# One core of attention plus a spectral mixer: placing the other work, the VectorE exponentials and the clock filler by a table of when engines and tiles come free

## The chip, the cores and the metric

The kernel runs on one core of a Trainium2 chip. The metric is the device time of one execution in microseconds. Engines are named as in the profile: PE (TensorE matmul), PEld (its weight load), DVE (VectorE), ACT (ScalarE), POOL (GpSimd), SP (SyncE, which issues most DMAs).

## What is computed

```
x: 2048 x 448;  16 heads of 28
qkv = x @ wqkv;  p = softmax(q k^T * 28**-0.5);  a = (p v) @ wo          # attention
X = rfft2(x);  X = X * (w_r + 1j*w_i);  b = irfft2(X)                    # spectral mixer
g = sigmoid(sum(x * gate_w));  out = g * a + (1 - g) * b
```

The attention has 16 heads x 2048 x 2048 exponentials. The two Fourier transforms are written as matmuls with constant matrices, 16 tiles per stage.

## The kernel before

The head loads x and the weights, transposes x, and makes the keys, the first queries and the first values. Then `attention` runs the main loop. The heads are taken four at a time (T = 0..3) and the queries 512 at a time (q = 0..3), so there are 16 chunks (T, q), and each chunk has 16 key blocks x 4 heads = 64 score tiles of 128 keys x 512 queries: 1,024 in all.

A step m of the loop handles three score tiles. `scores(m)` makes three matmuls into one PSUM tile `psS` (three banks, two such tiles in turn). `exps(m)` is one ACT instruction over the whole tile, which writes `Pt`. `values` multiplies finished `Pt` tiles by the values, eight at a time, into `psPV`. In some steps one of the three tiles is not given to ACT: `away` makes its exponential on DVE and POOL, as a chain: `bits` (DVE, reads psS), `frac` and a second `bits` (DVE), two `horner` operations on POOL, two `horner` on DVE, and `px` (DVE), which `values` then uses. The list `AWAY` gives 44 such tiles, at fixed places in each chunk, and the steps of a chain are emitted 0, 3, 4 and 5 steps after the tile.

Everything else is "other work", a list of units with due steps: the projections of the next keys and queries (`pkb`, `pn`, `pq`, `pq2`), the values (`pvp`), the Fourier stages (`psx1`, `psA`, `psT`, `psB`, `psZ`, `psY`) and the output tiles (`pf`). Each unit is a few matmuls into the one PSUM bank `bg` (`ps_bg`, one buffer), and a DVE operation that empties it. So a unit's first matmul waits until DVE has emptied the unit before.

All engines run strictly in the order of emission (`InOrder` keeps the program order). PE therefore meets, in each step: filler, scores of the next step, values, other work. The planner `other_work(m, room)` counts matmul columns: a step has `ROOM` = 1.22 us of PE time, filler, values and scores are taken off, and units are emitted while their columns fit in the rest. It knows nothing of when the bank, DVE or POOL come free. `filler` adds matmuls on a zero tile `warm`, with results that nobody reads, into the psS tile ahead of the scores; it wants 3 x `BUSY` = 4,950 columns over three steps. `need(key)` emits units without a limit when the next scores depend on them. The operations put in `later` for a step (chain steps, `normalise`) are emitted at the end of that step.

The functions that the change touches, and what calls them:

## Time and profile before

| | |
|---|---|
| runs, us | 490.14, 494.55, 493.25; median 493.25 |
| profiled execution: own time / span / granted clock | 490.54 us / 488.0 us / 0.986 |
| busy in the span | ACT 457.2 us (94%), PE 399.3 (82%), DVE 343.8 (70%), POOL 187.6 (38%) |
| start to first exponential | 18.48 us |
| first exponential to end of the last | 461.3 us (18.48 to 479.82) |
| from there to the end of the span | 8.2 us |
| exponentials on ACT | 297 of 128x1536, 44 of 128x1024, 1 of 128x512 |
| exponentials on DVE and POOL | 44 of 128x512 |
| filler matmuls in psS | 162 |

The span is what the profiler saw of one execution; that execution's own time is 2.5 us longer. Shares are averages over stages with different limits. In the lists, one row is a group of instructions: engine, operation, output <- input, shape, count, busy time, mean of one, and the idle time of the engine just before them with the instruction that ended it. Nearly every row has the line L128, a helper through which all operations are recorded, so rows are told apart by their tiles. Durations of neighbouring ACT instructions overlap a little: a 128x1536 exponential lasts about 1.45 us, but the next one starts 1.33 us after it.

### The profile page before, as it was taken

The page shows a single profiled execution, that of the slowest core. Times are in us where ns is not written, and L with a number is a line of the kernel's source. Part 1 is how long each engine was busy: PE and PEld are TensorE (multiplying, and loading weights), DVE is VectorE, ACT ScalarE, POOL GpSimd, SP SyncE. Part 2 cuts the span into 40 slices and gives each one's busy share as a digit, 9 for nine tenths or more (in the row PEclk, how much of TensorE's full clock was granted, in tenths as well). Part 3 has the DMA queues.
Part 4 walks back from the last instruction along what each step waited for, and adds up shares of the span by engine and source line. Part 5 has one row for each costly group of instructions (what it writes and reads, how often), then busy time and mean ns, then how long its engine had stood idle before and what let it go on. Part 6 is the DMA issues. An engine that isn't in the chain of part 4 may idle for free.

```text
span 488.0 us, 8101 instructions
## 1 busy us (share of the span) xinstructions
PE 399.3 (82%) x3162; PEld 148.2 (30%) x3164; DVE 343.8 (70%) x602; ACT 457.2 (94%) x364; POOL 187.6 (38%) x213
## 2 busy tenths in 40 slices
PE   8878878878898878787777778878878888888795
PEld 4422222222322233332333223333333233332221
DVE  4584766767585677877797677677867657686773
ACT  4899999999999999998999969999999899999993
POOL 3261625464222533435576652343224223222410
PEclk9999999999999999998999979999999899999999
DMA  8800000000000000001222100000000000100001
GB/s 251 198 2 1 1 1 0 1 1 1 2 1 1 1 0 1 0 10 46 51 56 51 54 2 0 3 1 11 23 22 11 23 1 31 49 13 21 20 28 48
DMA packets 15518, 12.69 MB, mean 26 GB/s; under 512 B 6984, under 2 KB 14600, under 8 KB 15480
## 3 DMA queue, kind: packets, MB, share of 16 engines
q1 hardware_dynamic: 14728, 11.91, 9.0%
q8 instruction: 24, 0.39, 0.3%
q10 hardware_dynamic: 752, 0.28, 0.2%
q14 instruction: 14, 0.11, 0.1%
HBM read 10.35 MB, written 1.84 MB: 25 GB/s over the span
## 4 chain that ended last, share of the span: by engine, by line
ACT 37%; PE 27%; DVE 20%; issue 14%; DMA 1%; POOL 0%; SPq 0%; DVEq 0%; ACTq 0%
ACT Pt L128 37%; PE psS L128 7%; PE psPV L128 6%; DVE bits L128 3%; PE psA L128 2%; DVE horner L128 2%; PE pkb L128 2%; DVE frac L128 2%; PE pf L128 2%; PE pq L128 2%; DVE U L128 2%; PE pvp L128 1%; DVE V L128 1%; DVE px L128 1%; DMA xtok<-in_A_x_dram 1%
## 5 line engine op out<-in xcount | busy, mean ns | idle before, releaser
L128 ACT ACTIVATE Pt<-psS 128x1536 bf16<-128x1536 f32 (+1 forms) x342 | 445.8, 1435 | 16.6 <-PE psS L128 15.1
L128 PE MATMUL psS<-qT,kT 32*128 32x512 bf16 x1024 | 135.9, 387 | 25.2 <-ACT Pt L128 22.7
L128 POOL TENSOR_SCALAR horner<-frac 128x512 f32<-128x512 f32 x44 | 37.3, 848 | 200.8 <-DVE frac L128 200.8
L128 PE MATMUL psPV<-Pt,vsb 128*32 128x512 bf16 x980 | 87.1, 390 | 0.1
L128 PEld LDWEIGHTS <-kT 32*128 32x128 bf16 x1024 | 38.3, 91 | 136.9 <-issue 125.7
L128 DVE SCALAR_TENSOR_TENSOR horner<-horner,frac 128x512 f32<-128x512 f32 x88 | 63.3, 719 | 2.6 <-POOL horner L128 1.8
L128 PE MATMUL psS<-warm 128*128 128x512 bf16 (+18 forms) x162 | 44.0, 325 | 17.6 <-ACT Pt L128 14.5
L128 POOL TENSOR_TENSOR horner<-horner,frac 128x512 f32<-128x512 f32 x44 | 55.7, 1266 | 3.7
L128 DVE TENSOR_SCALAR bits<-psS 128x512 int32<-128x512 f32 x44 | 30.2, 687 | 22.7 <-PE psS L128 22.5
L128 POOL TENSOR_TENSOR sq<-qr 128x512 bf16<-128x512 bf16 x16 | 19.6, 1227 | 41.7 <-DVE qr L128 41.7
L128 DVE SCALAR_TENSOR_TENSOR px<-horner,bits 128x512 bf16<-128x512 f32 x44 | 31.0, 705 | 0.6
L128 PEld LDWEIGHTS <-vsb 128*32 128x32 bf16 x1024 | 19.6, 94 | 35.3 <-issue 30.6
L128 PEld LDWEIGHTS <-warm 128*128 128x128 bf16 x188 | 17.8, 99 | 40.7 <-issue 26.5
L128 POOL TENSOR_TENSOR cm_t<-Xri,Wg 128x225 bf16<-128x225 bf16 x32 | 20.1, 648 | 15.7 <-DVE Xri L128 15.5
L128 DVE TENSOR_SCALAR frac<-bits 128x512 int32<-128x512 int32 x44 | 24.4, 554 | 0.1
L128 POOL TENSOR_TENSOR sq<-kT 128x512 bf16<-128x512 bf16 x12 | 15.7, 1304 | 20.4 <-DVE kT L128 20.3
L128 PEld LDWEIGHTS <-xT 112*128 112x128 bf16 x192 | 13.5, 97 | 24.1 <-issue 19.5
L128 DVE CAST ZT<-psZ 113x512 bf16<-113x512 f32 x16 | 11.0, 690 | 12.8 <-PE psZ L128 12.7
L128 DVE TENSOR_SCALAR bits<-bits 128x512 int32<-128x512 int32 x44 | 18.8, 427 | 1.5
L128 PE MATMUL pq<-xT,WqP 112*128 112x512 bf16 x64 | 17.9, 381 | 2.4 <-DVE V L128 0.9
L128 PE MATMUL pf<-WoP,qT 128*128 128x448 bf16 x60 | 15.1, 354 | 4.4 <-DVE part L128 1.6
L128 PE MATMUL psY<-Binv,ZT 113*128 113x448 bf16 x64 | 16.4, 367 | 2.6 <-DVE ZT L128 1.5
(90 smaller groups left out, 448.0 us busy)
## 6 DMA issues: line engine op xcount, KB each, us to landing
RBg<-cRB SPq DMA_DIRECT2D x16, 128.0 KB, 2.1
xtok<-in_A_x_dram SPq DMA_DIRECT2D x4, 448.0 KB, 4.6
out_dram<-fin SPq DMA_DIRECT2D x15, 112.0 KB, 1.7
CSg<-cCS SPq DMA_DIRECT2D x16, 96.0 KB, 1.9
Wg<-in_B_w_r_dram SPq DMA_DIRECT2D x16, 56.2 KB, 1.8
Wg<-in_B_w_i_dram SPq DMA_DIRECT2D x16, 56.2 KB, 2.0
Wqk<-in_A_wqkv_dram SPq DMA_DIRECT2D x1, 784.0 KB, 11.2
Binv<-cBinv SPq DMA_DIRECT2D x1, 448.0 KB, 13.4
```

Of the source, the lines that this page charges most:

```text
L128: return lambda *a, **k: self._tc.keep_in_program_order(f(*a, **k))
```

## The change

The planner's column count is replaced by a table, `Estimate`. At every emitted operation, `note` adds a cost (from shape and engine, by fixed formulas) to that engine's time, and records when the output is done, when inputs have been read, and so when a buffer comes free. The rest of the planner asks it:

- `other_work(m, limit)` emits a unit's next matmul only if the estimated start (PE free and the bg bank free) plus its cost is no later than `limit`, which is the estimated end of exponential m+1 less `GUARD` = 0.77 us. Several units may go into one step.
- The chain steps of `away` go into a queue. `steps_away`, called at the end of each step and after each finished unit, emits at most one, and holds it back if its input is not ready or if it would delay the emptying of the bg bank by the running unit (for at most `HOLD` steps).
- Tiles for DVE are chosen as the loop goes (`choose`): at least `GAP` = 4.2 us apart by the table, DVE free, no more than two chain steps waiting, none among the last 30 tiles of a chunk. `px` has five buffers where it had three. 39 tiles are chosen where the list had 44.
- `values` takes a `px` tile when the table says that it is ready, not a fixed eight steps later.
- `filler` wants 3,300 columns in the last 3.0 us by the table, where score matmuls count a third and value matmuls a quarter.

The core of the diff (pool wrappers that tell the table of new tiles, and renamed helpers, are left out):

```diff
-ROOM = 1.22
-ALLOW = 0.25
-SWITCH = 0.11
-BUSY = 1650
-UNIT = 1000
+BUSY = 3300
+UNIT = 400
+WINDOW = 3.0
+GUARD = 0.77
-AWAY = {c: [0, 5, 11] if c not in (7, 8) else [0] for c in range(16)}
-LAG = 8
+REST = 30
+GAP = 4.2
+HOLD = 4
+PXB = 5
...
+class Estimate:
+    def start(self, eng, names, out):
+        t = max(self.now[eng], self.free.get(out, 0.0))
+        return max([t] + [self.done[n] for n in names if n in self.done])
+    def columns(self, since):
+        return sum(c for t, c in self.moved if t > since)
+    def note(self, eng, op, args):
...
+        t = self.start(eng, ins, out)
+        late = 0.05
+        if eng == "PE":
+            kind = "u"
+            cols = P if op == "transpose" else n if len(aps) < 3 else int(np.prod(aps[2].shape[1:]))
+            cost = cols * MM
+            if aps[0].tensor.name.startswith("psS") and aps[1].shape[0] == 32:
+                kind, cost, cols = "s", 0.107, cols / 3.0
+            elif aps[0].shape[0] == 32:
+                kind, cost, cols = "v", 0.068, cols / 4.0
+            if kind == "u" and self.kind != "u":
+                cost += 0.09
+            self.kind, late = kind, 0.2
...
+        elif eng == "ACT":
+            cost, late = 0.06 + n * 0.833e-3, 0.13
+        elif eng == "DVE":
+            fast = op == "tensor_scalar" and len(aps) == 2 and aps[1].space != aps[0].space
+            fast = op == "tensor_scalar" and str(aps[1].space) == str(aps[0].space) and not fast
+            cost = 0.11 + n / (1920.0 if fast else 960.0)
+        else:
+            cost = 0.2 + n * 2.0e-3 if len(aps) > 2 else 0.13 + n * 1.3e-3
+        self.now[eng] = t + cost
...
-    def filler(self, m, room, base, ps):
-        want = 3 * BUSY - sum(self.activity[-2:]) - base - self.ahead(m, room)
-        fill = int(min(want, 900))
+    def filler(self, ps, ends):
+        t = self.est.start("PE", (), ps[:].tensor.name)
+        want = BUSY - self.est.columns(t - WINDOW)
+        fill = int(min(want, 900, (ends - t - 0.6) / MM))
...
+    def other_work(self, m, limit):
+        while True:
...
             key, g, cost = self.current
-            if cost > room:
-                break
+            if self.est.start("PE", (), self.bank) + cost > limit:
+                return
...
+    def steps_away(self, m, force=False):
+        est = self.est
+        while self.chain:
+            since, engine, ins, f = self.chain[0]
+            hold = m - since
+            t = est.start("DVE", ins, None)
+            if not force and hold < 2 * HOLD:
+                if t > est.now["DVE"] + 0.25 and t > est.now["PE"]:
+                    return
+                if self.current is not None and hold < HOLD:
+                    begun = est.start("PE", (), self.bank)
+                    if t + 0.6 > begun + self.left + 0.3:
+                        return
+            self.chain.pop(0)
+            f()
+            if not force:
+                return
...
+        def choose(m, t):
+            ci = acts[0][0]
+            if (len(self.chain) > 2 or t < self.last_away + GAP or len(out) >= PXB - 1
+                    or est.now["DVE"] > t + 0.3):
+                return None
...
+            if m + 1 in psS:
+                begin = max(est.now["ACT"], est.done[psS[m + 1][:].tensor.name])
+                limit = begin + 0.06 + len(tiles[m + 1]) * QW * 0.833e-3 - GUARD
+            else:
+                limit = est.now["ACT"]
+            self.other_work(m, limit)
+            self.steps_away(m)
```

## The prediction

> **What bounds the kernel now.** I read the page's busy table and its slices first, then the exponentials on ACT in order of time, then PE and DVE at the places where ACT had waited, then the granted clock there.

> ```profile
> PE 399.3 (82%) x3162; PEld 148.2 (30%) x3164; DVE 343.8 (70%) x602; ACT 457.2 (94%) x364; POOL 187.6 (38%) x213
> ACT  4899999999999999998999969999999899999993
> L128 ACT ACTIVATE Pt<-psS 128x1536 bf16<-128x1536 f32 (+1 forms) x342 | 445.8, 1435 | 16.6 <-PE psS L128 15.1
> ```

> ACT is the bound. It is full in nearly every slice, and where it waits, it waits for scores from PE. The span is 18.5 us of head, 461.3 us from the first exponential to the end of the last, and 8.2 us of tail. What would the middle be with no wait? In the trace the starts of undisturbed neighbours are 1.331 us apart after a 128x1536 and 0.904 after a 128x1024 (the longer "mean" is the duration, which overlaps the next). 297 x 1.331 + 44 x 0.904 + 0.5 = 435.6 us. So 25.7 us of the 461.3 are excess, and only this can be won. The page's 16.6 us of idle are less, since an idle gap counts only from the end of the duration, some 0.13 us later, and delays under 0.13 don't show.

> Where the excess lies (ACT in order of time, last bracket the idle time):

> ```profile
> 227.76 1.45 ACT L128 ACTIVATE Pt<-psS 128x1536 bf16<-128x1536 f32 x1 [1.46 <-PE psS L128]
> ...
> 280.92 2.37 ACT L128 ACTIVATE Pt<-psS 128x1024 bf16<-128x1024 f32 x2 [0.81 <-PE psS L128]
> 285.82 4.54 ACT L128 ACTIVATE Pt<-psS 128x1536 bf16<-128x1536 f32 x3 [2.54 <-PE psS L128]
> 291.30 1.45 ACT L128 ACTIVATE Pt<-psS 128x1536 bf16<-128x1536 f32 x1 [0.94 <-PE psS L128]
> ...
> 384.93 1.45 ACT L128 ACTIVATE Pt<-psS 128x1536 bf16<-128x1536 f32 x1 [1.27 <-PE psS L128]
> 387.01 1.45 ACT L128 ACTIVATE Pt<-psS 128x1536 bf16<-128x1536 f32 x1 [0.63 <-PE psS L128]
> ```

> Three bursts (with two more rows of 0.20 and 0.57 at 292.95 and 294.55) make 8.4 us of idle in 8 waits, with 0.13 each 9.5 us of excess. The other 16.2 us are some 60 delays of 0.1 to 0.6 us all over the loop. Now PE and DVE at the first two bursts:

> ```profile
> 225.79 0.57 PE L128 MATMUL pn<-sq,IS 128*128 128x512 bf16 x1 [1.71 <-DVE Xri L128]
> 284.26 0.91 PE L128 MATMUL psS<-warm 128*128 128x512 bf16 x2 [2.22 <-DVE bits L128]
> ```
> ```profile
> 223.51 1.69 DVE L128 SCALAR_TENSOR_TENSOR horner<-horner,frac 128x512 f32<-128x512 f32 x2
> 225.13 0.61 DVE L128 CAST Xri<-psB 128x450 bf16<-128x450 f32 x1
> ```

> PE isn't short of time, it stands in line: the emptying of the bg bank (Xri) queued on DVE behind two chain steps, a bg matmul on PE queued behind that, and the scores behind the matmul. The second burst is the same with `bits`, which holds the psS tile; the third is a ZT behind px, frac and bits. By the built order a step's PE work without filler is 0.84 us on average (a score matmul at 0.107, a value at 0.068, other columns at 2,400 per us), against 1.33 us of exponential, and only 8 of 341 steps hold more than 1.33.

> Then the clock around the bursts (PE busy, PEld, DVE, ACT, POOL, granted clock):

> ```profile
> 222.40:225.80 3.40, 1.69 (x19) 0.65 (x19) 3.30 (x7) 3.40 (x3) 2.18 (x3) 1.00 0.35 83
> 225.80:229.20 3.40, 3.40 (x20) 0.73 (x20) 3.33 (x7) 1.94 (x3) 2.39 (x3) 0.51 0.19 46
> 280.50:283.90 3.40, 1.54 (x11) 0.62 (x11) 3.23 (x6) 2.37 (x2) 3.32 (x5) 1.00 0.00 0
> 283.90:290.70 6.80, 6.20 (x27) 1.79 (x27) 4.18 (x8) 4.35 (x3) 2.28 (x3) 0.50 0.02 4
> 379.40:382.80 3.40, 2.09 (x20) 0.76 (x13) 3.22 (x5) 3.40 (x4) 2.45 (x3) 1.00 0.12 39
> ```

> Each burst is followed by 3.4 or 6.8 us at half clock. The windows before held 2,948, 2,026 and 3,374 matmul columns (scores counted a third, values a quarter). The four late exponentials inside the 6.8 us cost 1.8 us, so I price one half-clock window at 0.9 us.

> **The change, part by part.**

> *Fewer tiles on DVE.* 44 become 39 (counted in the built order). ACT takes five more tiles, in instructions that it issues anyway: 5 x (1.331 - 0.904) = +2.1 us on the path. DVE loses 5 x (0.687 + 0.554 + 0.427 + 2 x 0.719 + 0.705) = 19 us, POOL 5 x (0.848 + 1.266) = 11 us; neither is the bound, so this brings nothing by itself. The floor becomes 435.6 + 2.1 = 437.7 us.

> *Chain steps spread.* In the order before, DVE meets runs of three or more chain operations in a row 40 times, 15 of them within two neighbouring steps, the longest of six. After it is 9 times, 3 of them dense, the longest of four. This is the cause of the bursts. I take their 9.5 us down to 1; bounds 0 and 9.5.

> *Other work placed by the bank.* Of the 16.2 us of small delays some 2.1 are below 0.05 us each and stay. Nearly all others come a step or so after PE waited for DVE or stood in a filler. A unit's matmul now goes in only where bank and limit allow, so these go as far as the table is right. The limit leaves 0.77 us before the end of an exponential; three scores (0.32 us) and 0.2 us of latency need 0.52, so 0.25 us of error is absorbed. Where is the table wrong by more? It reckons DVE by the output's size:

> ```profile
> L128 DVE TENSOR_TENSOR cm_t<-Xri,Wg 128x225 bf16<-128x225 bf16 x32 | 14.7, 502 | 0.6
> L128 DVE TENSOR_REDUCE nm<-pn 128x1 f32<-128x512 f32 x16 | 10.9, 678 | 3.6 <-PE pn L128 3.6
> L128 DVE TENSOR_TENSOR G<-cm_t,cm_t 128x225 bf16<-128x225 bf16 x16 | 9.1, 569 | 0.6
> ```

> A minimum `nm` has an output of one element: 0.11 us in the table, 0.68 in the row. That is 0.57 - 0.25 = 0.32 us, at the 12 places inside the loop 3.8 us. A complex product has three DVE operations at 0.344 in the table, 0.54 us too little together; less 0.25, at 16 places, 4.6 us. At most 8.4 us, at least 0 (a unit need not follow at once); I take half, 4.2. Steps with more than 1.33 us of PE work are now 5, together 0.4 us over.

> *Less filler.* 162 matmuls become 65, and 60,010 columns 21,697. PE gains 97 x 0.272 (44.0 us / 162) = 26 us of idle time, worth nothing on the path. Its cover is the clock. The new aim, 3,300 columns in 3.0 us, is 3,750 in 3.41. With each step's columns spread over its exponential, 2 of the loop's 135 windows of 3.41 us lie below 3,400 in the order after (none before), and a tenth, 13, below 3,870. I take 2.5 windows at half clock, 2.2 us; bounds 0 and 13 x 0.9 = 11.7.

> [...]

> *Moved and unmoved.* Up to the first exponential all engines have the same instructions. SP issues the same DMAs in the same order, some steps earlier or later; they land in about 2 us on a queue that is mostly idle. At the end, two `pf` matmuls and a `fin` on DVE now stand between the last scores and the last values: +0.3 us, half of the 0.68 of a fin. The waits for `px` moved with the order, and it is still used 1 to 4 steps after it is made.

> **The sum.** Excess: 2.1 + 1 + 4.2 + 0.4 + 2.2 = 9.9 us. Span 18.5 + 437.7 + 9.9 + 8.2 + 0.3 = 474.6. The profiled execution's own time was 490.54 for a span of 488.0, so 474.6 is 477.1 of own time. The median of the three runs is 2.7 above that execution; with half of it I predict 478.5 us, 3.0% less than the median of 493.25.

> **The rivals.** (1) *The table is nearly right everywhere.* For it: the chains are thinned and PE has 0.5 us to spare in a mean step. Excess 2.1 + 0.4 + 1 = 3.5: 472 us. Against it are the two mis-sized DVE costs. (2) *The waits come back in the same amount.* There is still one bg bank with 216 handovers in one line on PE, and three neighbouring steps hold eight or more DVE operations 26 times, 22 before. Each DVE operation that the table prices too low makes the next evacuation late, unseen. With all 8.4 us, 5 us of remaining bursts and 7 half-clock windows (6.3): 2.1 + 8.4 + 5 + 0.4 + 6.3 = 22.2, which gives 491 us, no change. (3) *Slower: the clock.* PE with 97 fillers less hovers at the threshold, and half-clock windows follow each other. The price is 0.9 us each. Without the clock term the forecast is 476.3, so it decides from (498.2 - 476.3) / 0.9 = 24 windows of 135; with 30 the time is 503 us. For it: a window of 3,374 columns dropped, and the aim is only a tenth above. Against it: only about 2 windows are so low by order, and at half clock PE is busy throughout, which brought the full clock back after one or two windows each time.

> **How the numbers follow.** Forecast 0.55, nearly all rival 0.18, no change 0.17, clock 0.10. The range reaches from just below the first rival, 471, to the second, 491. This kernel's runs differ by about 1%, so 1% is what a measurement can tell from no change. Faster by more (below 488.3): 0.55 + 0.18 + a little of the second = 0.75; the same: 0.15; slower: 0.10.

> **What would show it.** In the profile after: 302 exponentials of 128x1536 and 39 of 128x1024; the idle time before Pt down from 16.6 to 4 to 6 us; no wait over 1 us of PE for Xri, ZT or bits; two to four half-clock windows; PE busy near 370 us. I am wrong if ACT's idle time stays near 16 us, and then the waits of PE tell which: behind `nm` and `G` it is the table's costs, at half clock without a wait before it the filler.

## The result, and the profile after

| | before, same chip | after |
|---|---|---|
| runs, us | 488.13 to 494.55, four runs | 533.18, 535.41, 545.24, 556.87; a fifth, 539.23, is in the ratio alone |
| median, us | 491.69 | 540.33 |
| ratio, 95% interval | | 1.0904 [1.0779, 1.1029] |
| first exponential to end of the last (profiled) | 461.3 us | 528.5 us |
| floor of that stretch, no wait anywhere | 435.6 us | 437.7 us |
| excess over the floor | 25.7 us | 90.7 us |
| half clock inside it | 13.7 us, 4 windows | 238.9 us, 70 windows |

The change makes the kernel 9% slower; the forecast was 478.5 us, 3% faster. The third rival, the clock, was right in its direction and in what carries the loss. The profiled execution of the kernel after is its slowest (556.87 us; the others ran at granted clocks of 0.82 to 0.85 against its 0.785), so its excess is some 16 us larger than the median's, and by their clocks the others spent an estimated 158 to 195 us at half clock, where it spent 239. The medians here count every execution; the ratios leave out those that are more than 1.5% above the fastest of their kernel.

The page of the kernel after, busy table, slices and the exponentials' group:

```profile
PE 466.8 (84%) x3067; PEld 150.8 (27%) x3067; DVE 335.1 (60%) x572; ACT 467.6 (84%) x364; POOL 173.8 (31%) x203
ACT  5888979788799867779897879877889799999994
PEclk9965968567689855559986558865879699999999
L193 ACT ACTIVATE Pt<-psS 128x1536 bf16<-128x1536 f32 (+1 forms) x342 | 456.2, 1435 | 73.3 <-PE psS L193 71.2
```

PE lost 95 instructions and yet is busy for 67 us more: the same matmuls took longer (a score matmul 466 ns on average, 387 before). The clock row shows why. Slices of 5 to 8 come again and again in the first four fifths of the span, and where that row stays low the ACT row is at 7 and 8. ACT's idle time in front of the exponentials is 73.3 us (16.6 before), and 71.2 of it is a wait for scores. The last fifth, where the clock stays at 9, is as full on ACT as the old kernel.

How one such stretch begins. The order of PE, then of DVE, after 187 us:

```profile
188.29 0.39 PE L193 MATMUL psS<-qT,kT 32*128 32x512 bf16 x3 [0.73 <-ACT Pt L193]
189.97 1.65 PE L193 MATMUL psx<-Bd,xT 112*128 112x450 bf16 x4 [1.29 <-DVE X L193]
191.55 1.03 PE L193 MATMUL psS<-qT,kT 32*128 32x512 bf16 x3
```
```profile
188.58 0.69 DVE L193 SCALAR_TENSOR_TENSOR horner<-horner,frac 128x512 f32<-128x512 f32 x1 [2.97 <-POOL horner L193]
189.19 0.24 DVE L193 RECIPROCAL rc<-oU 128x16 f32<-128x16 f32 x1
189.35 0.56 DVE L193 CAST X<-psx 128x450 bf16<-128x450 f32 x1
```

PE has nothing to do but to wait for the bg bank, which `X` on DVE empties, behind a `horner` that waited for POOL. These waits leave PE busy for 1.45 of 3.4 us. Then the table of stretches (us; PE, PEld, DVE, ACT, POOL busy; granted clock; DMA), with the window that did it, the stretch that followed, 50 us from inside it, and 50 us near the end:

```profile
186.50:189.90 3.40, 1.45 (x15) 0.39 (x8) 1.32 (x4) 3.40 (x4) 2.28 (x4) 1.00 0.00 0
189.90:251.40 61.50, 55.96 (x271) 18.11 (x270) 33.38 (x54) 42.63 (x31) 14.11 (x14) 0.50 0.00 1
200.00:250.00 50.00, 45.10 (x221) 14.94 (x220) 28.66 (x45) 35.96 (x27) 10.41 (x10) 0.50 0.00 1
450.00:500.00 50.00, 40.68 (x340) 14.65 (x332) 31.26 (x51) 49.96 (x40) 11.01 (x10) 1.00 0.09 26
```

The clock went to half at 190.0 and came back at 251.5 us, 18 windows of 3.41 us later. In those 61.5 us ACT began 30 exponentials, one in 2.05 us instead of 1.33. The third line is what the forecast had ruled out: PE is busy for 90% of the time, DVE for 57% and ACT for 72%, and the clock still doesn't return. PE was busy for 56.0 us in 30 steps, 1.9 us each, where the prediction counted 0.84 us of matmuls a step without filler at full clock. That is more than an exponential, so PE is the bound.

How much of the loss lies in such stretches can be read from the starts of the exponentials. Call what the spacing of two neighbours has over 1.331 us (0.904 after a 128x1024) the delay of a step. In the kernel after, 138 of the 341 steps begin or end at half clock, and they hold 81.6 us of delay; the 203 others hold 8.9 us, 0.044 us each. In the kernel before it is 8.0 us in 9 steps and 17.6 us in 332, 0.053 us each. So what the kernel after lost, it lost at half clock.

### The profile page after: what moved, and what is told of

The parts are those of the page before. It is cut to its first block, busy times and chain, and to the rows that moved or that the text cites. A ratio compares the mean times of both kernels' runs of the same rounds, so it can differ in the third digit from the quotient of the medians.

```text
span 555.1 us, 7865 instructions
## 1 busy us (share of the span) xinstructions
PE 466.8 (84%) x3067; PEld 150.8 (27%) x3067; DVE 335.1 (60%) x572; ACT 467.6 (84%) x364; POOL 173.8 (31%) x203
## 4 chain that ended last, share of the span: by engine, by line
PE 43%; ACT 25%; DVE 17%; issue 10%; POOL 4%; DVEq 0%; ACTq 0%; POOLq 0%
ACT Pt L193 25%; PE psS L193 13%; PE psPV L193 9%; PE psA L193 5%; PE pq L193 4%; PE pkb L193 3%; PE pvp L193 3%; POOL horner L193 2%; DVE horner L193 2%; DVE qT L193 2%; PE psx L193 2%; DVE cm_t L193 2%; DVE V L193 1%; DVE Xri L193 1%; DVE U L193 1%
## 5 line engine op out<-in xcount | busy, mean ns | idle before, releaser
L193 ACT ACTIVATE Pt<-psS 128x1536 bf16<-128x1536 f32 (+1 forms) x342 | 456.2, 1435 | 73.3 <-PE psS L193 71.2
L193 PE MATMUL psS<-qT,kT 32*128 32x512 bf16 x1024 | 170.6, 466 | 15.3 <-ACT Pt L193 12.0
L193 PE MATMUL psPV<-Pt,vsb 128*32 128x512 bf16 x985 | 101.2, 476 | 3.2 <-DVE oU L193 2.7
L193 POOL TENSOR_SCALAR horner<-frac 128x512 f32<-128x512 f32 x39 | 30.0, 770 | 141.2 <-DVE frac L193 140.3
L193 DVE SCALAR_TENSOR_TENSOR horner<-horner,frac 128x512 f32<-128x512 f32 x78 | 56.9, 729 | 9.7 <-POOL horner L193 9.2
L193 PE MATMUL psS<-warm 128*128 128x512 bf16 (+16 forms) x65 | 22.2, 382 | 9.6 <-ACT Pt L193 9.4
L193 POOL TENSOR_TENSOR on<-oU,rc 128x512 bf16<-128x512 f32 x15 | 16.6, 1105 | 26.9 <-DVE rc L193 26.9
L193 PEld LDWEIGHTS <-xT 112*128 112x128 bf16 x192 | 15.1, 104 | 32.3 <-issue 26.6
L193 DVE CAST qr<-pq 128x512 bf16<-128x512 f32 x16 | 11.0, 690 | 21.2 <-PE pq L193 21.2
L193 PE MATMUL pvp<-Wv,xT 112*128 112x336 bf16 x64 | 19.4, 418 | 4.1 <-DVE qT L193 2.1
L193 DVE CAST vsb<-pvp 128x336 bf16<-128x336 f32 x16 | 8.1, 508 | 21.9 <-PE pvp L193 21.9
## 6 DMA issues: line engine op xcount, KB each, us to landing
Binv<-cBinv SPq DMA_DIRECT2D x1, 448.0 KB, 13.7
```

Of the source, the lines that this page charges most:

```text
L193: r = self._tc.keep_in_program_order(f(*a, **k))
```

## The experiments

Kernels named "table" are built on the kernel after, "old" on the kernel before. "Fill" is the number of matmul columns that `filler` emits in the loop; the kernel before has 60,010, the kernel after 21,697. Half-clock windows are those of each profiled execution, the granted clock's time at half divided by 3.413 us; that execution can be far from the median (it is the fastest of e10, and the slowest of the kernel after, of e1 and of e9). Ratios are to the kernel before.

| run | fill | half-clock windows | median us | ratio [95%] |
|---|---|---|---|---|
| e1 table | 57k | 33 | 521.88 | 1.0638 [1.0554, 1.0723] |
| e2 table | 85k | 15 | 513.80 | 1.0493 [1.0418, 1.0568] |
| e3 old | 19k | 17 | 495.20 | 1.0102 [1.0036, 1.0168] |
| e4 table | 0 | 62 | 534.72 (one run) | |
| e5 e2, inputs and minima priced | 88k | 20 | 521.96 | 1.0701 [1.0610, 1.0792] |
| e6 table, guard 0.5 | 66k | 11 | 508.78 | 1.0384 [1.0302, 1.0466] |
| e7 e6, inputs and minima priced | 65k | 22 | 518.50 | 1.0577 [1.0484, 1.0671] |
| e8 table | 118k | 19 | 531.53 | 1.0858 [1.0774, 1.0942] |
| e9 table places other work only | 65k | 27 | 506.83 | 1.0294 [1.0225, 1.0363] |
| e10 table's chains only | 53k | 6 | 496.84 | 1.0033 [0.9970, 1.0096] |
| e11 e6, filler not cut | 68k | 25 | 533.42 | 1.0864 [1.0792, 1.0937] |
| e12 e10 + table places other work | 54k | 22 | 514.84 | 1.0480 [1.0417, 1.0544] |
| e13 e10 + table's filler rule | 49k | 16 | 501.66 | 1.0209 [1.0151, 1.0266] |
| e14 e6, one unit a step | 67k | 28 | 519.89 | 1.0542 [1.0458, 1.0626] |
| e15 old | 69k | 5 | 490.68 | 0.9971 [0.9930, 1.0013] |
| e16 e10, units need both conditions | 50k | 12 | 496.32 | 1.0075 [1.0007, 1.0144] |
| e17 e16, more filler | 64k | 11 | 495.50 | 1.0098 [1.0044, 1.0152] |

The medians of e5, e6, e8, e10, e12, e14 and e17 lie outside every range that was named for them, so what follows rests on comparing runs with each other.

### Is it the missing filler? (e1 to e4, e8, e15)

The aim of the filler is changed, first in the new order, then in the old.

```diff
-BUSY = 3300
+BUSY = 4100        # e1;  4500 in e2, 5000 in e8
```

> The table's order as changed, but its filler aim raised from 3,300 to 4,100 columns in 3.0 us: 167 filler matmuls, 57.0 thousand columns, where the changed kernel has 65 and 21.7 thousand and the old one 162 and 60.0 thousand. Theory A (the loss is the half clock, and the half clock comes from the filler that was taken out): granted clock back to 0.96 or more, ACT's idle time before Pt from 73 to under 15 us, time 476 to 490 us. Theory B (the table's order itself makes PE stand in line behind DVE, and the half clock follows from those waits): clock under 0.92, time over 505 us.

> The same with the aim at 4,500 columns: 239 filler matmuls, 85.0 thousand columns, more than the old kernel. Theory A: clock 0.98 or more, time 474 to 486 us, the price of the order alone, to be held against the 478.5 that I forecast. Theory B: as in the run with 57 thousand, over 505 us. A third reading (filler stands before the scores on PE and costs by itself): clock near 1, but time over 495 us.

> The table's order with the filler aim at 5,000 columns: 336 filler matmuls, 118 thousand columns; five projections of queries are forced. If the clock were all of the loss, the granted clock would rise over 0.97 and the time fall under 500 us. If the order has its own loss through forced units (C1), the clock rises, but the time stays at 508 to 520 us, since filler takes the place that late units need.

```diff
-BUSY = 1650
+BUSY = 1350        # e3 (old kernel);  1720 in e15
```

> The old order, but its filler aim lowered from 3 x 1,650 to 3 x 1,350 columns: 51 filler matmuls, 18.6 thousand columns, a little under the changed kernel's 65 and 21.7. Nothing else changes. Theory A: the old order loses its clock too: granted clock 0.75 to 0.90, time 515 to 550 us. Theory B: clock over 0.95 and time within 2% of the kernel before.

> The old order with its filler aim raised from 3 x 1,650 to 3 x 1,720: 201 filler matmuls, 69 thousand columns. By the built order no window of 3.41 us falls under 3,400 columns of the whole array. If the clock is what is left to win in the old order: 0.995 or more, and 1 to 4 us less than before; if filler costs as much as it keeps: within 0.5%.

```diff
         fill = int(min(want, 900, (ends - t - 0.6) / MM))
-        if fill < 96:
-            return
+        return                                                # e4
```

> The table's order with no filler in the loop at all (the other matmuls on the zero tile, in head and tail, stay). Theory A: clock 0.60 to 0.75, time 560 to 600 us, at a price of about 1.1 us for each 3.4 us at half clock. Theory B: time as the changed kernel's, 530 to 560 us, since the 65 filler matmuls do little.

Filler is at most half of the answer. With about as much filler as the old kernel (e1, 57k) the new order still loses 6.4% of the 9.0%, and at the best amount tried in it (e2) 4.9%. The reverse cut is the cleanest number of the set: the old order with a third of its filler (e3) has 17 half-clock windows where it had 4, and loses 1.0%. So some 41k columns less cost the old order 1.0%, and 35k less, from e1 to the kernel after, cost the new one 2.5% (1.0904 / 1.0638). The last 65 fillers of the kernel after bring nothing that shows: without any (e4) one execution took 534.72 us, within the spread of its own runs. At 118k columns (e8) the loss is larger again. Its steps at full clock have 0.12 us of delay each against 0.09 in e2, which fits filler that stands before the scores; but e8 also has five forced projections against three (see below), and the two were not separated. And the old amount was enough for the old order (e15 is the same).

### Which waits? (e2 read closely, then e5, e6, e7, e14)

In e2 the longest wait of ACT in the last part of the loop is 5.2 us (timeline, the PE weight loads left out):

```profile
468.39 1.02 PE L193 MATMUL pq<-xT,WqP 112*128 112x512 bf16 x4 [0.77 <-DVE bm L193]
...
469.45 0.69 DVE L193 CAST qr<-pq 128x512 bf16<-128x512 f32 x1 [1.11 <-PE pq L193]
...
470.22 1.04 POOL L193 TENSOR_TENSOR sq<-qr 128x512 bf16<-128x512 bf16 x1 [10.62 <-DVE qr L193]
...
471.58 0.39 PE L193 MATMUL pq<-sq,IS 128*128 128x512 bf16 x1 [0.79 <-DVE ZT L193]
472.00 0.75 DVE L193 SCALAR_TENSOR_TENSOR qT<-pq,nhk,qr 128x512 bf16<-128x512 f32 x1 [0.48 <-PE pq L193]
...
472.81 0.39 PE L193 MATMUL psS<-qT,kT 32*128 32x512 bf16 x3 [0.84 <-DVE qT L193]
...
473.31 2.37 ACT L193 ACTIVATE Pt<-psS 128x1536 bf16<-128x1536 f32 x2 [5.20 <-PE psS L193]
```

This is `need`: the next queries were not ready, because the limit with its guard of 0.77 us had let other work fall behind, so the projection ran as one line PE, DVE, POOL, PE, DVE with ACT empty. By the built orders this happens to an unfinished projection once in the kernel after, three times in e2, five times in e5 and e8, and not at all in e6 and e7, where the guard is 0.5 us (once in e9, e11 and e14, which have that guard too). Four edits tried the placing itself. One lets units go later, two give the table what the prediction said it lacked, one allows a single unit per step:

```diff
-GUARD = 0.77
+GUARD = 0.5                                                   # e6, e7, e14; BUSY = 4500 in all four
...
+        if op == "tensor_reduce":                             # e5, e7
+            n = int(np.prod(aps[1].shape[1:]))
...
+            self.ins = (st["sq"][:].tensor.name,)             # e5, e7: before pq2 and pn
...
-            if self.est.start("PE", (), self.bank) + cost > limit:
+            if self.est.start("PE", self.ins, self.bank) + cost > limit:
...
                 self.steps_away(m)
+                return                                        # e14: after a finished unit
```

> The table's order at the filler aim of 4,500 (513.8 us so far), with two holes of the table mended: the limit also asks when the squares on POOL (sq) that the second projection units (pq2, pn) read are done, and a minimum is priced by its 512 inputs. By the build, five projections of queries are still not finished when the scores need them, and are then emitted at once without a limit (three in the run at 4,500). Theory C1 (such late units, forced out in one line through PE, DVE, POOL, PE, DVE, are the order's main loss): 510 to 520 us. Theory C2 (the holes are the main loss): under 503 us.

> The table's order at the aim of 4,500, with GUARD 0.50 us instead of 0.77: other work may run until 0.50 us before the estimated end of an exponential. By the build no unit is forced any more; filler falls to 184 matmuls, 66 thousand columns, since other work takes its place. Theory C1: the loss of the order mostly goes, under 503 us, and no wait of ACT over 2 us. Theory C3 (the limit already lets other work too near to the end, so that every error of the table reaches ACT): slower than 513.8, over 518 us.

> Both of the above together: no forced unit, inputs on POOL and minima known to the table. C1 alone: as the run with GUARD 0.50, within 1%. C1 and C2: 3 to 10 us less than it, under 495 us. C3: over 510 us.

> The run with GUARD 0.50 and aim 4,500 (508.8 us), with at most one unit finished per step, as the old planner had it; one projection of queries is forced. If units that follow each other in one step are what costs, since the second stands behind the emptying of the bank: under 498 us. If it is that work runs on until shortly before the exponential's end: 503 to 515 us.

Without the forced projections, and with less filler, e6 is 5 us faster than e2 by the medians, though the intervals overlap. The right price of a minimum and the wait for `sq` made things worse in both pairs (e5 against e2, e7 against e6, the second pair with no forced projection in either). So the mis-sized minimum, one of the prediction's two reasons for waits that would stay, is not what makes the order slow. The other, the price of the complex product (`cm_t` and `G`), was not corrected in any run. Nor is it that units come several to a step: e14 is no better than e6.

### The halves of the planner exchanged (e9, e10, e12, e13, e11)

e9 keeps the table for other work and filler, and puts the DVE tiles and their chain steps back to the old fixed places. e10 is the reverse: the table chooses DVE tiles, chain steps and the use of `px`, while other work and filler go by the old column count. e12 and e13 then add one part each to e10.

```diff
-        self.chain += [(m, "DVE", (bits[:].tensor.name,), fraction), (m, "DVE", (), power),
...
+        for d, f in ((0, fraction), (0, power), (3, lambda: times(POLY[2], v, h)),
+                     (4, lambda: times(POLY[1], v, h)), (5, last)):
+            self.later.setdefault(m + d, []).append(f)        # e9
```
```diff
-            self.other_work(m, limit)
+            used += self.by_room(m, self.room + ALLOW - self.over - used, self.base)   # e10
...
-        want = BUSY - self.est.columns(t - WINDOW)
+        want = 3 * 1650 - sum(self.activity[-2:]) - base - self.ahead(m, room)         # e10
```
```diff
-            used += self.by_room(m, self.room + ALLOW - self.over - used, self.base)
+            self.other_work(m, limit)                         # e12, on e10; GUARD = 0.5
...
```
```diff
-        want = 3 * 1650 - sum(self.activity[-2:]) - base - self.ahead(m, room)
-        fill = int(min(want, 900))
...
+        want = BUSY - self.est.columns(t - WINDOW)            # e13, on e10; BUSY = 3900
+        fill = int(min(want, 900, (ends - t - 0.6) / MM))
```
```diff
-        fill = int(min(want, 900, (ends - t - 0.6) / MM))
+        fill = int(min(want, 900))                            # e11, on e6; BUSY = 4000
```

> The table places other work and filler (aim 4,500, GUARD 0.50, as in the run at 508.8 us), but the DVE tiles stand at the old fixed places, 44 of them, their chain steps are emitted 0, 0, 3, 4 and 5 steps after the tile and px is used 8 steps after it, as before. One projection unit is forced, by its last matmul. If the placing of other work is the loss: 503 to 518 us, as the run with both. If the placing of the chains and of px is the loss: under 498 us.

> The other half: other work and filler by the old count of columns (one unit at most per step, 142 filler matmuls, 53 thousand columns), but the DVE tiles, their chain steps and the use of px chosen by the table; 45 tiles for DVE. If the placing of other work was the loss, this is no slower than the kernel before: 474 to 490 us, and what is below 488 is what my term for the spread chains is worth (8.5 us forecast). If the chains' placing was the loss: over 498 us.

> Only the rule for other work from the table (limit with GUARD 0.50, several units in a step), with the old rule for filler (148 matmuls, 54 thousand columns) and the table's chains; no unit is forced. It differs from the run with the old work and the table's chains (496.8 us, ratio 1.003 to before) in the placing of other work alone. If that placing is the loss: 500 to 512 us, and the median distance by which scores are ready ahead of their exponential under 0.33 us (0.46 there). If it was the filler rule: under 494 us.

> The opposite: other work by the old count of columns, the table's chains, and the table's filler rule (columns in the last 3.0 us, cut to the room before the end of the exponential) at an aim of 3,900: 140 matmuls, 49 thousand columns; no unit is forced. If the placing of other work is the loss: 484 to 497 us. If it was the filler rule: 500 to 512 us.

> As the run with GUARD 0.50, but the filler is no longer cut down to the room that the table sees before the end of the running exponential; its aim is 4,000 so that its amount stays (188 matmuls, 68 thousand columns against 184 and 66). If the cut takes filler away just after PE has waited, when the clock needs it: granted clock over 0.975 and time under 500 us. If not: 503 to 515 us, or more, since filler now also stands before late scores.

The part that costs most is the placing of other work. The table's chains alone (e10) are as fast as before by the ratio, within 1%, but less steady: its ten executions took 488.7 to 509.9 us, the longer the lower their clock (0.979 down to 0.913), where the kernel before never took more than 495.2, and by the medians e10 is 1.2% slower. Adding the table's placing of other work, with the old filler rule and about the same amount (54k), costs 4.5% (1.0480 / 1.0033, e12; 3.2% by the medians). Adding the table's filler rule costs 1.8% (1.0209 / 1.0033, e13; 49k columns against 53k), but 0.6% by the medians, so that one is not clear. The table's chains aren't needed for the loss: with the old ones, e9 still loses 2.9%. The cut of the filler is not the fault: without it (e11) the kernel is slower still.

What does the placing do? The exponentials' groups, and what PE (the first of its rows) and ACT waited for, with the total, the number of waits and the longest; first e10, then e12:

```profile
L194 ACT ACTIVATE Pt<-psS 128x1536 bf16<-128x1536 f32 (+1 forms) x342 | 444.6, 1440 | 16.4 <-PE psS L194 15.1
...
PE psS L194 <- ACT Pt L194: 41.5, 105, 0.8
PE pq L194 <- POOL sq L194: 3.1, 4, 1.1
...
ACT Pt L194 <- PE psS L194: 15.1, 23, 2.0
```
```profile
L194 ACT ACTIVATE Pt<-psS 128x1536 bf16<-128x1536 f32 (+1 forms) x342 | 450.1, 1409 | 38.0 <-PE psS L194 36.6
...
PE psS L194 <- ACT Pt L194: 21.9, 53, 0.9
PE pq L194 <- POOL sq L194: 5.7, 5, 2.2
PE psPV L194 <- DVE oU L194: 4.5, 5, 1.4
...
ACT Pt L194 <- PE psS L194: 36.6, 57, 1.9
```

In e10 PE waits 105 times for ACT to free the score tile: it has come early, and this wait is harmless. In e12 it does so half as often, and ACT waits for PE 57 times instead of 23. Summing PE's idle time in the loop by what the next matmul is, over the traces:

| | PE idle, us | before other work | gaps over 0.7 us there | before scores or their filler |
|---|---|---|---|---|
| before | 81.5 | 39.0 | 11 | 42.4 |
| e10 | 82.4 | 36.0 | 12 | 45.1 |
| e12 | 88.9 | 58.1 | 20 | 26.3 |
| e6 | 84.2 | 53.6 | 17 | 27.4 |
| after | 81.2 | 53.2 | 18 | 24.5 |

PE stands idle for about as long everywhere. What the placing changes is where: some 15 to 20 us move from in front of the scores, where PE waits for a tile that ACT still holds, to in front of other work, where the scores stand behind it in line. In steps at full clock the scores are finished 0.39 us (median) before their exponential could start in the kernel before and 0.46 us in e10, but 0.30 in e12 and 0.26 in e6, which have a guard of 0.5 us. In the kernel after, with its guard of 0.77 us, it is 0.39 as before. The limit in `other_work` permits the move, as its code reads: it asks that a unit *end* before the exponential does, less the guard, and counts the time that PE stands at the bank as free. The delay of the steps, as defined above, shows what came of it:

| | steps at full clock | delay there, us | a step | steps that begin or end at half clock | delay there, us |
|---|---|---|---|---|---|
| before | 332 | 17.6 | 0.053 | 9 | 8.0 |
| e10 | 328 | 14.2 | 0.043 | 13 | 10.3 |
| e12 | 295 | 22.8 | 0.077 | 46 | 28.3 |
| e6 | 317 | 23.8 | 0.075 | 24 | 16.4 |
| e2 | 305 | 27.0 | 0.089 | 36 | 18.8 |
| after | 203 | 8.9 | 0.044 | 138 | 81.6 |

From e10 to e12 the delay grows by 26.6 us, 18.0 of it at half clock (an upper value, since the profile of e10 is of its fastest execution) and 8.6 at full clock. With the most filler or a smaller guard (e2, e6) the order pays in both ways; the kernel after pays at half clock alone. A wait that a half-clock window follows is counted here where the next exponential starts, mostly at half clock.

### Both conditions (e16, e17)

If so, a unit that must fit into the old column count *and* be seen by the table to end 0.30 us before the exponential should keep the lead.

```diff
-            if cost > room:
+            if cost > room or self.est.start("PE", (), self.bank) + cost > limit:      # e16, on e10
...
-        want = 3 * 1650 - ...
+        want = 3 * 1720 - ...                                 # e17, on e16
```

> Old filler rule and the table's chains, as in the runs at 496.8 and 514.8 us, but a unit's matmul is emitted only if both rules allow it: the old count of columns has room for it, and the table sees it end 0.30 us before the exponential's end. No unit is forced; 138 filler matmuls, 50 thousand columns. If the loss comes from the work that the table allows beyond the old count (PE then stands at the bank while nothing else is emitted): the time falls back to 484 to 497 us, and PE's idle time before other work from 58 us (in the run at 514.8) to under 42. If the table's estimates are so wrong that its limit does harm by itself: over 500 us.

> The same with the filler aim at 3 x 1,720 columns: 176 filler matmuls, 64 thousand columns. It is the best version that the runs point to: if the spread chains and the table's limit are worth anything, 478 to 486 us, below both kernels; if neither is, 486 to 493.

The loss of e12 is gone (1.0480 to 1.0075), with a looser guard, and PE's idle time is back in its old places (35.8 us before other work, 43.9 before scores). So the column count, which also allows one unit a step at most, keeps the order good, and the table's condition on top of it wins nothing: e16 and e17 are both a little slower than before. No version here beat the old kernel; e15 is the same within 1%, and so is e10 by its ratio.

## Why the prediction was wrong, point by point

**The floor, right.** 302 exponentials of the wide and 39 of the narrow form, as counted; +2.1 us. The ends outside the loop stayed as before (8.2 us after the last exponential), so the 0.3 us added there didn't come. What failed is the excess: 9.9 us forecast, 90.7 in the profiled execution.

**"Less filler", the step that failed.** It stood in the sum with 2.2 us: 2.5 windows at half clock, 0.9 us each. The profiled execution has 70 windows, and the steps that touch them hold 81.6 us of delay, 1.17 us a window. So the price was somewhat low (the prediction's own formula for the third rival makes 476.3 + 70 x 0.9 = 539.3 of the 556.87), and the count was wrong by far. It is made of two factors: the clock fell 14 times inside the loop, and each time it stayed down for five windows on average.

The falls were undercounted by an even spread: each step's columns were spread over its exponential, though real windows hold a wait and then a crowd; the window at 186.5 held 15 matmuls. They were also put down to the filler alone, though the clock falls with the old filler rule too once the table places the work (22 windows in e12, 6 in e10). The stays were ruled out by "at half clock PE is busy throughout, which brought the full clock back". That rested on three returns in the trace of before. In the trace after, the clock returned after 14 of 70 windows, though PE was busy for 94% of them on average. The weights, a score as a third, matter less: with them the windows of the traces sort almost as well as with a quarter, at a bound of 3,140 to 3,280 columns, and the prediction took 3,400.

**"Other work placed by the bank", not there.** 16.2 us of small delays were to shrink to 4.2. Without its clock term the forecast has 7.7 us of excess, 0.023 us a step; at full clock the kernel after has 0.044, little less than before (0.053). And the placing alone costs 4.5% in an order with the old filler rule (e12), in waits of ACT that go from 15.1 to 36.6 us. I had taken the bank's wait as what placing removes. It doesn't remove it (PE idle is 82.4 us in e10 and 88.9 in e12), it moves it to in front of other work, on an engine that runs in order with the scores behind. The table's price for `nm` was a wrong suspect (e7 against e6); that for `G` was not put to the test.

**"Chain steps spread", not there.** 9.5 us of bursts were to go. With the chains spread and nearly all else as before, e10 is within 1% of the old kernel by the ratio, and its profile has the same 15.1 us of waiting for scores as the old one. The bursts read in the trace were real, but other waits stand where they were: the longest wait in e10 is 2.0 us, in before 2.5.

**A wait that was not priced.** The forced projection: 5.2 us at one place of e2, and once in the kernel after by the built order.

**The rivals.** The third was right in what carries the loss, the half clock, and in its point of decision (24 windows). It got 0.10, because the even count above saw two low windows. Its condition, 97 fillers less, is only part of the cause: e1 has about the old amount of filler and 33 half-clock windows. And it is not all of the order's loss: e2 and e6 have 15 and 11 half-clock windows, lose 4.9 and 3.8%, and some 45% of the delay that they have over the kernel before lies at full clock (9.4 of 20.2 us, 6.2 of 14.6). That split is read from one trace of each; no run holds the clock and changes the order alone. A second bank for other work was not tried, and no run shows whether it would take the wait itself away.

**What was to show it.** PE's waits behind `ZT` and `Xri` reached 1.4 us where none over 1 us was expected, and "at half clock without a wait before it the filler" was the wrong test: here the two act together. More filler in the new order (e2) and the old placing with the old filler rule (e10) each bring the windows down from 70, to 15 and to 6.

## What to carry to other kernels

A planner that knows when a resource comes free may plan to *wait* for it; on an engine that runs in order the wait is charged to whatever stands behind (ACT waited 36.6 us for scores in e12, 15.1 in e10), so limit the engine's time in a step as well as the moment at which a unit ends. Filler and order have one price together: before filler is cut, count windows in real time and by the share of the array, and ask whether a step's work still fits at half clock, for if not, one dropped window can last for tens of microseconds (61.5 us here, where a step held 1.9 us of PE time). When a change has several parts, exchange them one by one between old and new: four such runs told here what two traces of the whole could not.

## What the runs showed of the hardware

| window | followed by | number | columns | PE busy, median |
|---|---|---|---|---|
| full clock | half clock | 159 | 754 to 3,171, 90% under 2,894 | 54% |
| full clock | full clock | 2,095 | 90% over 3,475 | 85% |
| half clock | half clock | 266 | median 2,760, 90% under 2,999 | 93% |
| half clock | full clock | 159 | median 3,207, 90% over 3,031 | 100% |

So for this mix one bound near 3,000 columns serves both ways: it misplaces 27 of the 2,254 windows at full clock and 35 of the 425 at half clock, where the best bound on PE's busy time misplaces 51 and 112. At half clock 512-column matmuls in a row start 0.38 to 0.43 us apart (kernel after; at full clock 0.215 to 0.227), and a PE that is never idle can stay below the bound: in 202 windows at half clock PE was busy for over 99.5% of the time, and after 80 of them the clock stayed at half. The bound is fitted to these windows and was not tried on others.
